# Two transformer layers on one core: scores of one head pair and maxima of another in one visit to the PSUM banks

## The chip, the cores and the metric

The kernel runs on one core of a Trainium2 chip. The metric is the time of one execution on the device in microseconds, median of three runs. The core has five engines with a queue each: TensorE (PE; its weight loads are listed as PEld), VectorE (DVE), ScalarE (ACT), GpSimd (POOL) and SyncE (SP), which here issues most DMAs. Each engine takes its own instructions in order, and semaphores tie the engines together.

## The reference

Two layers on x of 2048 rows and 640 columns. Each layer is attention with a sliding window of 256 keys (32 heads of 20 columns) and a feed-forward with squared ReLU (1536 wide):

```python
def _A_ref(x, wqkv, wo):
    H = 32; Dh = D // H; W = 256
    ...
    scores = jnp.einsum("bhqd,bhkd->bhqk", q, k) * (Dh ** -0.5)
    mask = (idx[:, None] - idx[None, :] >= 0) & (idx[:, None] - idx[None, :] < W)
    scores = jnp.where(mask[None, None], scores, -1e9)
    p = _softmax(scores, axis=-1)
    o = jnp.einsum("bhqk,bhkd->bhqd", p, v)
    return (...o...) @ wo
def _B_ref(x, w1, b1, w2, b2):
    h = jnp.einsum("bsd,df->bsf", x, w1) + b1
    r = jnp.where(h > zero, h, zero)
    return jnp.einsum("bsf,fd->bsd", r * r, w2) + b2
...
x = x + _A_ref(_layernorm(x), A_wqkv, A_wo)
x = x + _B_ref(_layernorm(x), B_w1, B_b1, B_w2, B_b2)
x = x + _A_ref(_layernorm(x), A_wqkv, A_wo)
x = x + _B_ref(_layernorm(x), B_w1, B_b1, B_w2, B_b2)
```

## The kernel before

The rows are cut into units of 256; two layers make 16 units (`NU`), numbered u. A unit is u % 8 == 0 at the start of a layer, where no earlier keys exist. Every dense product is done on fp16 high and low halves: `mm3` (L322) sums three products for each chunk of 128, high times high, high times low, low times high. Dense work of a unit is the query and key projection (`stage_qk`), the value projection (`stage_v`), the output projection (`stage_o`) and the feed-forward (`stage_f`), in that order of data. Dense groups accumulate in one of two PSUM tiles of the tag "mm"; ACT or DVE empties a tile before it is used again. The values and the small transposes use the same two tiles.

Attention works by head pairs: 16 pairs in a unit, 8 quads of two pairs. One head of a pair sits in rows 0 to 63, the other in rows 64 to 127 (index e), so a score matmul is a 64x64 tile of PE. Six PSUM banks, `bb6`, three for each e, hold scores. They are used twice for each quad:

- `max_quad` (L616) computes the scores of a quad with queries on the partitions (L652, or L667 at the start of a layer) and posts eight DVE reductions (L632), which add a mask, take the row maxima and write the masked scores back in place into the banks. A reduction shows as two DVE instructions, the reduction and a read of the accumulator into `mx`. The maxima are turned by a DMA (`max_cross`) or by PE (`max_out`) and appended as two extra rows of the queries. Maxima run `LEAD` = 3 quads ahead of the scores that need them.
- `exp_quad` (L736) computes the scores with keys on the partitions and with the maximum already subtracted by the two extra rows (L756, or L764 without 64-column tiles). ACT takes the exponential of each bank (L778: six of 512 columns a quad) into SBUF tiles `pt`, and POOL zeroes what the window excludes (L793, L797).

`pv_quad` (L813) multiplies the masked exponentials with the values (L827), four heads side by side in 32-column tiles; ACT copies the result to `ot` (L839) and SP stores it to DRAM (L844). `load_o` reads it back in the layout that the output projection needs and divides by the row sums.

The order of each engine's instructions is written by the program itself: a planner with its own clock `now` posts a job for each ACT, DVE, POOL and SP instruction with an estimated cost, and PE's work is emitted as the planner's clock goes on. `together` (L1092) walks a unit's quads: scores of quad n, a share of the dense stream, maxima of quad n+3 and then values of quad n, the rest of the share. Before scores or maxima it goes on with dense work until the jobs that use the banks (`bbjobs`) have ended by the planner's clock. `flow` (L1156) does the same for the first unit. In the last two units part of the dense work is held back (`CARRY`, `KEEP`) for the stretch behind the last values, where the output projection waits for `load_o`.

## Time and profile before

| | |
|---|---|
| median of 3 runs | 1591.49 us (1591.14 to 1591.74) |
| the profiled execution | 1590.84 us, of which the span of its instructions is 1589.1 us |
| PE | 1558.1 us busy |
| DVE, ACT, POOL | 983.8, 735.2, 599.5 us busy |
| granted TensorE clock, mean | 0.997 |

The page names an instruction by its line, engine and operation, then the tile it writes and the tiles it reads. Busy time of PE includes the modelled end of each matmul; two groups' starts are the better measure of what a group costs. A bracket behind a timeline row gives the idle time of that engine just ahead of the row, and whose signal ended it.

### The profile page before, as it was taken

How to read it: one execution, taken by the hardware profiler on the slowest of the kernel's cores; microseconds unless marked ns; L12 is line 12 of the kernel's file. 1: busy time of each engine (PE TensorE's matmuls, PEld its weight loads, DVE VectorE, ACT ScalarE, POOL GpSimd, SP SyncE). 2: the span in 40 equal slices, each digit the busy share in tenths (PEclk: the TensorE clock that was granted, in tenths of full speed). 3: DMA queues.
4: the chain of work that ended last, by engine and by line, in shares of the span. 5: the costliest groups of instructions: out<-in, count | busy, mean ns of one | idle time of the engine just before them, and what ended most of it. 6: DMA issues, size and time to landing. Idle time of an engine off the chain costs nothing.

```text
span 1589.1 us, 52465 instructions
## 1 busy us (share of the span) xinstructions
PE 1558.1 (98%) x21534; PEld 1167.5 (73%) x21534; DVE 983.8 (62%) x3253; ACT 735.2 (46%) x1593; POOL 599.5 (38%) x1291
## 2 busy tenths in 40 slices
PE   8989999999999999999999999999999999999999
PEld 7666767777777777778777777777777777776767
DVE  8787665656756656665566656557665665756432
ACT  4555535444453444535343453544545345454522
POOL 1234424334252443525323352442535235353512
PEclk9999999999999999999999999999999999999999
DMA  9763243362533525343362535434343352441020
GB/s 273 206 181 100 70 121 81 100 129 52 121 87 103 110 65 130 69 127 84 97 133 57 122 83 123 92 88 111 69 123 83 98 123 64 111 83 58 29 67 18
DMA packets 243209, 160.44 MB, mean 101 GB/s; under 512 B 91160, under 2 KB 226712, under 8 KB 242968
## 3 DMA queue, kind: packets, MB, share of 16 engines
q1 hardware_dynamic: 236600, 147.58, 38.8%
q10 hardware_dynamic: 6368, 9.50, 2.0%
q8 instruction: 169, 2.77, 0.7%
q14 instruction: 72, 0.59, 0.1%
HBM read 84.68 MB, written 52.95 MB: 87 GB/s over the span
## 4 chain that ended last, share of the span: by engine, by line
PE 91%; DVE 3%; ACT 2%; DMA 2%; SPq 1%; issue 1%; POOL 0%; ACTq 0%; DVEq 0%; POOLq 0%
PE acc L327 70%; PE pv L827 11%; PE bb L652 5%; PE bb L756 5%; DVE bb L632 1%; ACT pt L778 1%; DMA o<-ot 0%; PE bb L764 0%; DMA ov<-o 0%; PE bb L667 0%; SPq L688 0%; DVE qd L509 0%; DVE mx L632 0%; DMA qt<-qk 0%; DMA qk<-qd 0%
## 5 line engine op out<-in xcount | busy, mean ns | idle before, releaser
L778 ACT ACTIVATE pt<-bb 128x512 f32<-128x512 f32 (+1 forms) x736 | 376.9, 603 | 221.8 <-PE bb L756 198.9
L632 DVE CUSTOM_DVE_ANT_0 bb<-bb,maskq 128x320 f32<-128x320 f32 x896 | 409.2, 525 | 95.3 <-PE bb L652 88.6
L793 POOL TENSOR_SCALAR_AFFINE_SELECT pt<-pt 128x256 f32<-128x256 f32 x448 | 188.0, 422 | 558.1 <-ACT pt L778 545.3
L327 PE MATMUL acc<-y,w_s 128*128 128x256 f16 x2880 | 327.9, 273 | 2.1 <-ACT y L377 1.4
L327 PE MATMUL acc<-w_s,hh 128*128 128x320 f16 x2304 | 326.2, 299 | 0.0
L327 PEld LDWEIGHTS <-w_s 128*128 128x128 f16 x2880 | 276.6, 98 | 53.5 <-issue 17.7
L327 PEld LDWEIGHTS <-hh 128*128 128x128 f16 x2304 | 220.5, 98 | 98.4 <-issue 11.5
L327 PEld LDWEIGHTS <-wq_s 128*128 128x128 f16 x2400 | 230.0, 98 | 46.5 <-issue 13.8
L327 PE MATMUL acc<-yT,wq_s 128*128 128x256 f16 x2250 | 259.5, 273 | 2.1 <-DVE qd L509 0.7
L797 POOL TENSOR_SCALAR_AFFINE_SELECT pt<-pt 128x256 f32<-128x256 f32 x512 | 213.5, 438 | 89.2 <-ACT pt L778 87.6
L1012 DVE TENSOR_TENSOR hh<-r,hh 128x256 f16<-128x256 f32 x192 | 94.6, 513 | 213.2 <-ACT hh L1009 206.0
L827 PE MATMUL pv<-pt,vt 128*32 128x128 f32 (+1 forms) x3840 | 191.9, 330 | 0.7 <-POOL pt L797 0.6
L1006 POOL TENSOR_TENSOR r<-r 128x256 f32<-128x256 f32 x192 | 114.3, 615 | 169.5 <-ACT r L1002 167.2
L839 ACT COPY ot<-pv 128x256 f32<-128x256 f32 x128 | 47.8, 373 | 270.0 <-PE pv L827 266.1
L632 DVE DVE_READ_ACCUMULATOR2_ANT mx<- 128x1 f32 x1024 | 145.9, 143 | 0.0
L327 PE MATMUL acc<-wo_s,od 128*128 128x320 f16 x960 | 140.0, 301 | 3.8 <-ACT od L910 3.2
L827 PEld LDWEIGHTS pv<-pt,vt 128*32 128x32 f32 x3840 | 105.4, 109 | 42.1 <-POOL pt L797 6.9
L327 PE MATMUL acc<-wq_s,yT 128*128 128x320 f16 x900 | 131.8, 299 | 1.0 <-DVE y L378 0.5
L327 PEld LDWEIGHTS <-od 128*128 128x128 f16 x960 | 91.7, 98 | 48.7 <-issue 6.9
L1002 ACT ACTIVATE r<-acc,b1s 128x256 f32<-128x256 f32 x192 | 80.9, 473 | 95.9 <-PE acc L327 95.1
L327 PEld LDWEIGHTS <-yT 128*128 128x128 f16 x900 | 85.7, 98 | 39.2 <-issue 6.8
L364 POOL TENSOR_TENSOR bmv<-bmv,neghalf 128x1 f32<-128x1 f32 x64 | 44.2, 696 | 141.3 <-DVE bmv L358 140.8
(95 smaller groups left out, 1225.5 us busy)
## 6 DMA issues: line engine op xcount, KB each, us to landing
qt<-qk SPq DMA_DIRECT2D x30, 480.0 KB
kt<-qk SPq DMA_DIRECT2D x30, 480.0 KB
qk<-qd SPq DMA_DIRECT2D x17, 640.0 KB
o<-ot SPq DMA_DIRECT2D x256, 42.0 KB
od<-o SPq DMA_DIRECT2D x14, 640.0 KB
qk<-yl SPq DMA_DIRECT2D x13, 640.0 KB
qk<-qd SPq DMA_DIRECT2D x17, 320.0 KB
xt<-in_A_x_dram SPq DMA_DIRECT2D x16, 320.0 KB
```

Of the source, the lines that this page charges most:

```text
L327: nc.tensor.matmul(acc, lhs(a, c), rhs(b, c), start=(k == 0), stop=(k == 3 * nk - 1))
L632: nc.vector.tensor_tensor_reduce(out=v, in0=v, in1=mask, scale=1.0, scalar=-3.0e38, op0=ALU.add, op1=ALU.max, accum_out=accum[e, w]),
L652: nc.tensor.matmul(flat[e][rows, o:o + b - a], qt[r, p, i * P + 64 * h:i * P + 64 * (h + 1)], kt[r, p, a + to:b + to], start=True, stop=Tr ...
L756: nc.tensor.matmul(bb[e][rows, k, o + a:o + b], kt[r, 2 * qd + j, ko + 64 * h:ko + 64 * (h + 1)], qt[r, 2 * qd + j, q0 * P + a:q0 * P + b] ...
L778: nc.scalar.activation(box["pt"][:, :o], bb[e][:, k, :o], AF.Exp, scale=SCALE / (QS * QS))
L793: nc.gpsimd.affine_select(out=m, in_=m, pattern=[[0, 2], [-1, P]], compare_op=ALU.is_gt, fill=0.0, base=0, channel_multiplier=1)
L797: nc.gpsimd.affine_select(out=m, in_=m, pattern=[[0, 2], [1, P]], compare_op=ALU.is_ge, fill=0.0, base=0, channel_multiplier=-1)
L827: nc.tensor.matmul(pv[32 * jj:32 * (jj + 1), q0 * P:(q0 + qn) * P], vf[:, c:c + 32], pj[:, j, :], start=(k == 0), stop=(k == len(steps) - ...
L839: nc.scalar.copy(ot[:, qd % 2], pv)
L1002: nc.scalar.activation(box["r"], acc[:, f, :], AF.Relu, bias=b1s[:, f0 + f:f0 + f + 1], scale=1.0 / (YS * WS))
L1006: nc.gpsimd.tensor_tensor(box["r"], box["r"], box["r"], op=ALU.mult)
L1012: nc.vector.tensor_sub(hh[:, 1, f, :], box["r"], hh[:, 0, f, :])
```

## The change

The step is now a visit, one pair long instead of a quad. A visit computes the scores of one pair into columns 0 to 767 of the three banks of each e (0 to 383 at the start of a layer), and right behind them the scores for the maxima of a pair six ahead, into columns 768 to 1407 (1024 to 1407 at the start of a layer). A visit posts two exps of up to 768 columns and four reductions. The reductions write into two small SBUF tiles, `junk`, instead of the banks. At every second visit, ahead of the scores, come the values of the quad that the two visits before completed.

```diff
-    def max_quad(n):
+    GP = 2 * GQ
+    def max_pair(n):
...
+            def put():
+                j = junk[len(junked) % 2]
+                junked.append(0)
+                nc.vector.tensor_tensor_reduce(out=j[:, :cols], in0=v, in1=mask, scale=1.0, scalar=-3.0e38,
+                                               op0=ALU.add, op1=ALU.max, accum_out=acc)
...
-                p, at = 2 * qd + j, 5 * Q * w
-                cuts = sorted({0, 5 * Q, *(z - at for z in (512, 1024) if 0 < z - at < 5 * Q)})
+            places = [(i, 6 * P + 5 * Q * i) for i in range(2)]
+            for i, at in places:
+                cuts = sorted({0, 5 * Q, *(z - at for z in (1024,) if 0 < z - at < 5 * Q)})
...
-    def exp_quad(n):
+    def exp_pair(n, quad):
...
+        steps = [(3, cur, P, 1, 1), (2, cur, 0, 0, 2)]
+        if u % NG:
+            steps = [(1, prev, P, 0, 2), (0, prev, 0, 0, 1)] + steps
+        cols = sum(s[4] for s in steps) * P
...
-                    box["pt"] = sb.tile([P, 512], F32, name="pt", tag="pt", bufs=6)
-                    nc.scalar.activation(box["pt"][:, :o], bb[e][:, k, :o], AF.Exp, scale=SCALE / (QS * QS))
+                box["pt"] = sb.tile([P, 768], F32, name="pt", tag="pt", bufs=4)
+                nc.scalar.activation(box["pt"][:, :cols], bb[e][:, :cols], AF.Exp, scale=SCALE / (QS * QS))
...
     def pv_quad(n, quad):
+        need(*[j for _, ms in quad for j in ms])
...
-            ots[u] = sb.tile([P, 2, T], F32, name="ot", bufs=2)
+            ots[u] = sb.tile([P, 2, T], F32, name="ot", bufs=1)
...
-    LEAD = GQ + 1
+    LEAD = 6
...
+        for k, n in enumerate(ns):
+            m = ms[k] if k < len(ms) else None
...
+            work(k, Want(*wants, bank=full))
+            if full:
+                pv_quad(*hang.pop())
+            if not hang:
+                hang.append((n // 2, []))
+            banks()
+            exp_pair(n, hang[0][1])
             if m is not None:
-                max_quad(m)
+                max_pair(m)
...
-    QKC, VC, OC, FCST, LNC, CARRY, KEEP, MID = 16.4e3, 8.2e3, 8.2e3, 39.2e3, 1.2e3, 15e3, 20e3, 8e3
+    QKC, VC, OC, FCST, LNC, CARRY, KEEP, MID = 16.4e3, 8.2e3, 8.2e3, 39.2e3, 1.2e3, 20e3, 24e3, 8e3
...
-    spin(14)
+    spin(13)
...
-    spin(7)
+    spin(4)
...
-    run(some(dense, 10e3), stage_o(NU - 1), some(dense, 4e3))
+    flush(dense)
+    run(some(dense, 7e3), stage_o(NU - 1), some(dense, 4e3))
```

`flow` is rewritten by pairs in the same way, and `stage_o` may now wait for a `load_o` that the planner has not yet posted. Apart from attention, the first block of the first unit's query projection and the first block of the last feed-forward take all chunks of one product ahead of the next product, and their transposed operand is cut into four tiles, so that each product depends only on the pieces it reads:

```diff
-    def mm3(acc, lhs, rhs, nk, ns, then=None):
+    def mm3(acc, lhs, rhs, nk, ns, then=None, whole=0):
...
+        terms = ((0, 0), (0, 1), (1, 0))
+        if whole:
+            terms = [[t] for t in (terms if whole == 1 else terms[::2] + terms[1:2])]
+        for c, part in ([(c, part) for part in terms for c in range(nk)] if whole else [(c, terms) for c in range(nk)]):
...
+    def pieces_of(*tiles):
+        return lambda a, c, n, m: tiles[2 * a + c // 3][:, c % 3:c % 3 + n, m]
```

On PE, in the middle of the program, a quad's maxima (L652) were followed by its values (L827) and then by dense work (L327). `bb_133` and `bb_134` are the banks of e = 0 and 1, `kt` keys, `qt` queries, `vt` values:

```order
L652 LDWEIGHTS qt
L652 MATMUL bb_134<-kt_86,qt 64x192
L827 MATMUL pv<-pt,vt_93 32x256 [waits DVE_49,Pool_49]
L827 MATMUL pv<-pt,vt_93 32x256 [waits Pool_49]
L827 MATMUL pv<-pt,vt_93 32x256 x2
L827 MATMUL pv<-pt,vt_92 32x128 [waits Pool_49] x2
```

Now the values (L823 of the changed kernel) are followed by a pair's scores (L777):

```order
L823 MATMUL pv<-pt,vt_91 32x256 [waits DVE_49,Pool_49]
L823 MATMUL pv<-pt,vt_91 32x256 [waits Pool_49] x3
L823 MATMUL pv<-pt,vt_90 32x128 x4
L823 MATMUL pv<-pt,vt_93 32x128 x3
L823 MATMUL pv<-pt,vt_93 32x128 [waits Pool_49]
L823 MATMUL pv<-pt,vt_92 32x256 x4
L777 LDWEIGHTS kt_86
L777 MATMUL bb_133<-qt,kt_86 64x192
```

The values moved from behind the maxima to ahead of the scores, and the scores of the visit run straight on into its maxima (L678), with no dense work and no wait between:

```order
L777 MATMUL bb_133<-qt,kt_87 64x192
L777 LDWEIGHTS kt_87
L777 MATMUL bb_134<-qt,kt_87 64x192
L678 LDWEIGHTS qt
L678 MATMUL bb_133<-kt_87,qt 64x256
```

On DVE, the reductions of a quad stood in one row of eight behind a wait for PE:

```order
L632 ISA bb_133,mx<-bb_133,maskq 128x320 [waits PE_49]
L632 ISA mx 128x1
L632 ISA bb_134,mx<-bb_134,maskq 128x320 [waits PE_49]
L632 ISA mx 128x1
L632 ISA bb_133,mx<-bb_133,maskq 128x320 [waits DVE_49]
```

Now four stand together (L658), other work goes between the fours, and the first two wait for ACT:

```order
L1016 TENSOR_TENSOR hh<-r,hh 128x256 [waits Activation_49]
L658 ISA junk_135,mx<-bb_133,maskq 128x320 [waits Activation_49]
L658 ISA mx 128x1
L658 ISA junk_136,mx<-bb_134,maskq 128x320 [waits Activation_49]
L658 ISA mx 128x1
L658 ISA junk_135,mx<-bb_133,maskq 128x320 [waits DVE_49]
```

What moved is the signal that releases the first reduction of each bank: from PE's to ACT's, whose exp of the same visit reads the same banks.

## The prediction

> **What bounds the kernel now.** I read the page's first part first, then the windows, then the PE timeline of a stretch in the middle, then the waits.

> ```profile
> span 1589.1 us, 52465 instructions
> PE 1558.1 (98%) x21534; PEld 1167.5 (73%) x21534; DVE 983.8 (62%) x3253; ACT 735.2 (46%) x1593; POOL 599.5 (38%) x1291
> 0.00:160.00 160.00, 144.69 (x1638) 107.06 (x1639) 126.22 (x417) 84.51 (x173) 44.53 (x91) 0.98 0.69 189
> 160.00:240.00 80.00, 77.07 (x1149) 56.36 (x1148) 52.32 (x169) 36.28 (x78) 29.74 (x68) 0.98 0.40 96
> 240.00:1370.00 1130.00, 1129.97 (x16077) 851.32 (x16076) 698.44 (x2332) 525.10 (x1142) 441.15 (x961) 1.00 0.42 97
> 1370.00:1500.00 130.00, 124.05 (x1936) 90.24 (x1935) 81.02 (x282) 64.52 (x143) 61.87 (x132) 1.00 0.28 68
> 1500.00:1590.00 90.00, 82.28 (x741) 62.51 (x741) 25.80 (x56) 24.78 (x59) 22.25 (x40) 1.00 0.12 39
> ```

> A window row gives its length, then busy time of PE, PEld, DVE, ACT and POOL. The reader is to see that between 240 and 1370 us PE is busy for 1129.97 of 1130 us. PE's idle time lies at the two ends: 15.3 us before 160, 2.9 up to 240, 6.0 in 1370 to 1500, and 7.7 after 1500 (each the length less the first number). These 32 us are all that better waiting can give. DVE and ACT, which the change relieves most, are at 62% and 46%; in the long middle a faster DVE buys nothing. The first 160 us differ: DVE is busy for 126 of them.

> A busy PE may still lose time between its kinds of work, so the middle is read from the timeline: start, then the busy time of the group. One group's start to the next group's start is its price.

> ```profile
> 701.44 0.75 PE L756 MATMUL bb<-qt,kt 62*64 62x192 f16 x32
> 702.12 3.16 PE L327 MATMUL acc<-wq_s,yT 128*128 128x320 f16 x22
> 705.12 2.20 PE L327 MATMUL acc<-wo_s,od 128*128 128x320 f16 x15
> 707.25 0.76 PE L652 MATMUL bb<-kt,qt 60*64 60x256 f16 x38
> 707.94 1.51 PE L827 MATMUL pv<-pt,vt 128*32 128x256 f32 x32
> 709.38 4.25 PE L327 MATMUL acc<-wo_s,od 128*128 128x320 f16 x30
> ```

> A quad's scores (L756) cost 0.68 us, its look-ahead scores for maxima (L652) 0.69, its values (L827) 1.44. Dense matmuls cost 3.00 / 22 = 0.136 us each, and the 15 ahead of 707.25 take 2.13 instead of 2.04: 0.09 us to leave the dense shape. Nothing here waits; it is work.

> **The change, part by part.** Changes of shape: before, one quad is dense, scores, dense, maxima, values, dense. After, per two visits: dense, values, scores+maxima, dense, scores+maxima. PE leaves its dense shape twice per quad either way; "maxima to values" and "values to dense" give way to "values to scores" and "maxima to dense". Priced by the rows above these are equal, so 0. Scores to maxima has no row; both are 64-column tiles on 60 or 62 rows, so I take 0, with 0.09 us as the upper end, the row for leaving a shape. [...]

> Matmuls: the new places (columns 768 and 1088 of a three-bank row) need 18 maxima matmuls a pair, 36 a quad instead of 38. At (0.68 + 0.69) / 70 = 0.02 us a matmul the most that this gives is 0.04 us a quad, the least nothing. I take 0.027, times the 112 quads with 64-column tiles: **-3 us** (0 to -4.4).

> Turn-round of the banks: today maxima wait for all exps of a quad.

> ```profile
> PE bb L652 <- ACT pt L778: 8.9, 8, 2.7
> PE bb L756 <- DVE mx L632: 0.6, 3, 0.2
> 201.47 0.75 PE L756 MATMUL bb<-qt,kt 62*64 62x192 f16 x32
> 202.31 3.05 ACT L778 ACTIVATE pt<-bb 128x512 f32<-128x512 f32 x6 [3.13 <-PE bb L756]
> 204.93 0.27 PE L652 MATMUL bb<-kt,qt 60*64 60x256 f16 x1 [2.70 <-ACT pt L778]
> ```

> In all 8.9 us, eight times, where too little dense work lay between the two (here none). After the change scores and maxima go to different columns in one visit, so this wait is gone: **-8.9 us**. In its place the next visit's scores wait for this visit's exps and reductions. Its length:

> ```profile
> L778 ACT ACTIVATE pt<-bb 128x512 f32<-128x512 f32 x704 | 367.7, 612 | 221.8 <-PE bb L756 198.9 <-PE bb L764 15.7 <-DVE x L1040 4.0
> L778 ACT ACTIVATE pt<-bb 128x256 f32<-128x256 f32 x32 | 10.8, 398 | 0.0
> L797 POOL TENSOR_SCALAR_AFFINE_SELECT pt<-pt 128x256 f32<-128x256 f32 x512 | 213.5, 438 | 89.2 <-ACT pt L778 87.6 <-POOL pt L797 0.4
> 709.00 0.53 DVE L632 CUSTOM_DVE_ANT_0 bb<-bb,maskq 128x320 f32<-128x320 f32 x1
> 709.45 0.53 DVE L632 CUSTOM_DVE_ANT_0 bb<-bb,maskq 128x320 f32<-128x320 f32 x1
> 711.69 0.48 DVE L938 SCALAR_TENSOR_TENSOR x<-acc,x 128x320 f32<-128x320 f32 x1
> 712.09 0.87 DVE L353 BATCH_NORM_STATS2 bst<-x 128x6 f32<-128x320 f32 x2
> ```

> 256 more columns cost an exp 612 - 398 = 214 ns, so one of 768 takes 0.83 us; six of 512 follow each other at 3.05 / 6 = 0.51 us, so two of 768 at 0.72. A reduction that writes PSUM follows the last at 0.45 us; a DVE instruction of as many columns that reads PSUM and writes SBUF lets the next start after 0.40 (711.69 to 712.09). The new reductions write SBUF: I take 0.40, with 0.45 as the other end. Signalling: the scores that start at 201.47 end at 202.15, the exp starts at 202.31, 0.16 us later.

> In the order the first two reductions of a visit stand behind the visit's exps (waits Activation). So after a visit's last matmul: 0.16, exps until 0.16 + 0.72 + 0.83 = 1.71, 0.16, three reductions, 0.16: 3.2 us. If exps and reductions ran side by side, 0.16 + 4 x 0.40 + 0.16 = 1.9. Against it stand the slots of dense matmuls between visits. In the middle the shortest is 23 of 0.136 = 3.1 us once a unit, the next 28 (3.8 us); with other work in the queues I take 0.13 us a unit, **+1.5** (0 to 3). In the last two units some nine slots have 15 to 20 matmuls, 2.0 to 2.2 us, and lack up to 1.0 each: **+6** (0 to 9.4, the sum of what each lacks to 3.2). In the first unit slots of 15 of 0.109 = 1.6 us meet exps of 384 columns and reductions of 128 and 256, about 2.1 us by the same rows; seven such slots: **+1.5** (0 to 3).

> The values still wait for POOL: two masks behind each of the last pair's exps, 1.71 + 0.16 + 2 x 0.44 = 2.7 us after the visit, and values follow at least 28 dense matmuls (3 us) later: 0, covered by that dense work. In the last unit this cover is thin, which the range holds.

> The ends: the first block of the first projection now takes its operands in the order in which they are made, and so does the last feed-forward's first block.

> ```profile
> 10.80 0.39 PE L327 MATMUL acc<-yT,wq_s 128*128 128x256 f16 x2 [0.24 <-ACT wq_s L259]
> 11.82 0.94 PE L327 MATMUL acc<-yT,wq_s 128*128 128x256 f16 x7 [0.63 <-DVE wq_s L260]
> 1545.31 0.27 PE L327 MATMUL acc<-y,w_s 128*128 128x256 f16 x1 [1.40 <-ACT y L377]
> 1546.17 1.03 PE L327 MATMUL acc<-y,w_s 128*128 128x256 f16 x8 [0.60 <-DVE y L378]
> ```

> The DVE halves (0.63 and 0.60) are needed 10 matmuls (1.1 us) later and so hidden, and part of the 1.40, since the last block starts from a piece of the operand: **-2** (-1.2 to -2.6).

> DVE in the first 160 us: about 150 reductions fall there, each 0.05 us shorter, 7.5 us of DVE's 126. Only part stands where PE waits for DVE: **-3** (0 to -7.5).

> The single output buffer of the values (two before) makes the copy of every second quad wait for the stores of the quad before, issued a quad's 12 us earlier:

> ```profile
> 709.54 0.37 ACT L839 COPY ot<-pv 128x256 f32<-128x256 f32 x1 [2.49 <-PE pv L827]
> 709.94 1.35 SPq L844 DMA_DIRECT2D o<-ot  x4
> ```

> All four are issued within 1.8 us of the copy, so 10 us remain to land: 0. Without that cover ACT would stand, and PE two groups later.

> **The sum**: -3 - 8.9 + 1.5 + 6 + 1.5 - 2 - 3 = -7.9 us on the span of 1589.1, so 1581.2. The profiled run took 1590.84, 1.7 us over its span, and the median is 1591.49; taken off the median: **1584 us** (0.5% faster).

> **The rivals.** *Exp and reduction in one bank.* Columns 512 to 767 (exp) and 768 to 1023 (maxima) share a bank, and the order makes the second engine wait. A reduction at DVE's head, held 1.0 us by the first exp and 0.3 by the second, holds the evictions behind it too, whose banks the dense work needs. DVE's middle load is 698 of 1130 us, 7.4 of a quad's 12; two visits add up to 2.6 us and save 0.4, so on average DVE keeps up. But in the first 160 us some 30 visits of 1 us each bring 126 - 7.5 + 30 = 149 of 160. It decides where slots lie under 3.2 us: all new waits at their upper ends (15.4), no gain from DVE at the start and 7 us lost there, plus 0.5 us a unit for late evictions (6.5): -3 - 8.9 + 15.4 - 2 + 7 + 6.5 = +15, **1606 us**. For it: the waits in the order; against it: the room in the middle. [...]

> *Waits only change place*: the new waits eat the 8.9 and DVE's relief comes to nothing: -3 - 8.9 + 12 - 2 = -2, **1590 us**. For it: the ends have a fixed amount of dense work to cover with.

> *Scores to maxima costs a change of shape*: 0.09 us twice a quad, 112 x 0.18 = +20 on the sum: **1604 us**. Against it: both use 64-column tiles.

> *No new wait appears*: -3 - 8.9 - 2 - 5 = -19, **1572 us**, if the planner's spacing holds and DVE's relief counts at the start.

> **How the numbers follow.** Forecast 0.42 (its own range 1575 to 1588), no new wait 0.12, waits change place 0.14, the shared bank 0.27, the change of shape 0.05. About 0.2%, 3 us, is what a measurement of this kernel can tell from no change. Faster: 0.41 + 0.12 + 0.04 = 0.57; same: 0.01 + 0.09 = 0.10; slower: 0.27 + 0.05 + 0.01 = 0.33. The range takes in the bounds of both signs, from "no new wait" to the shared bank: 1570 to 1607.

> **What would show it.** Right: PE fully busy between 240 and 1370; no wait of maxima for exps; scores plus maxima 0.67 to 0.69 us a visit; reductions 0.40 us apart; waits of scores for reductions under 10 us in all, at the two ends. The shared bank shows as idle DVE ahead of reductions put down to ACT, and PE waiting in the middle; a change of shape as visits of 0.76 us or more. I am wrong if PE's idle time in the first 160 us grows, or if PE idles in the middle.

## The result and the profile after

The changed kernel takes **1633.09 us** (median of five runs, 1628.13 to 1636.51) against 1591.49: a ratio of 1.0256, 95% interval 1.0243 to 1.027. It is slower by 2.6%, where 0.5% faster was forecast, and 26 us above the upper end of the range. Its profiled execution took 1634.25 us, 1632.5 of it the span.

The windows of the changed kernel, columns as before (length, then PE, PEld, DVE, ACT, POOL busy; granted clock, DMA share, GB/s):

```profile
0.00:160.00 160.00, 132.83 (x1379) 93.93 (x1380) 117.00 (x391) 76.19 (x147) 31.63 (x75) 0.94 0.69 186
160.00:240.00 80.00, 76.24 (x1112) 56.65 (x1112) 44.46 (x157) 36.49 (x68) 32.46 (x70) 0.98 0.32 81
240.00:1370.00 1130.00, 1113.36 (x15664) 837.56 (x15662) 675.50 (x2296) 523.58 (x961) 431.00 (x947) 1.00 0.40 96
1370.00:1500.00 130.00, 123.65 (x1859) 89.53 (x1861) 76.73 (x273) 58.37 (x101) 50.35 (x116) 1.00 0.34 84
1500.00:1632.00 132.00, 120.15 (x1316) 90.12 (x1306) 50.61 (x140) 44.70 (x94) 42.73 (x84) 1.00 0.12 36
```

PE now idles in the middle: 1130 - 1113.36 = 16.6 us, where it had none. In the first 160 us it idles 27.2 us instead of 15.3, and its clock there is 0.94 instead of 0.98, which takes at most another 160 x 0.04 = 6.4 us (an estimate, as if PE had work all that time). DVE is not the busy engine: 117.00 us in the first 160 instead of 126.22, 675.50 in the middle instead of 698.44.

The spans differ by 43 us. Where these lie can be read from starts on PE's timeline (us from the span's start; e3 and e12 are experiments below):

| | before | after | e3 | e12 |
|---|---|---|---|---|
| first feed-forward matmul of unit 1 | 251.1 | 267.8 | 254.0 | 249.4 |
| the same of unit 12 | 1304.1 | 1338.7 | 1307.4 | 1299.8 |
| last matmul of the program | 1585.1 | 1628.5 | 1592.8 | 1581.3 |
| one unit in the middle | 96.58 | 98.16 | 96.48 | 96.18 |

So 16.7 us are lost ahead of the first row, 17.9 between the first two (1070.9 instead of 1053.0), and 8.8 behind.

The waits of the changed kernel (engine, tile and line that waited, whom for: us in total, times, longest):

```profile
DVE junk L658 <- ACT pt L794: 375.7, 380, 3.7
ACT pt L794 <- PE bb L678: 163.0, 153, 4.3
PE pv L823 <- DVE x L1045: 9.3, 12, 1.4
PE acc L330 <- DVE qd L526: 8.1, 11, 0.7
PE bb L777 <- DVE mx L658: 4.9, 11, 1.0
```

The first row is new. In the kernel before, of the 95.3 us that DVE stood idle ahead of its reductions of 320 columns, 1.1 were put down to an exp:

```profile
L632 DVE CUSTOM_DVE_ANT_0 bb<-bb,maskq 128x320 f32<-128x320 f32 x896 | 409.2, 525 | 95.3 <-PE bb L652 88.6 <-ACT r L1002 4.2 <-ACT pt L778 1.1
```

Now DVE stands 375.7 us with a reduction at the head of its queue that waits for an exp, 375.7 / 380 = 0.99 us each time. The last row is the wait that the prediction priced, scores waiting for reductions, and it is small. PE's large new waits are the third and fourth row: the values wait for the addition that empties the second feed-forward's bank (L1045), and the value projection waits for the second half of the query projection's eviction (L526). Within the middle they come to 8.2 and 7.4 us, ten times each: nearly all of the 16.6. One of them in the timeline (accumulator reads are left out):

```profile
719.88 0.47 PE L777 MATMUL bb<-qt,kt 62*64 62x192 f16 x16
720.19 0.46 PE L678 MATMUL bb<-kt,qt 60*64 60x256 f16 x18
720.58 3.45 PE L330 MATMUL acc<-yT,wq_s 128*128 128x256 f16 x30
720.83 1.51 ACT L794 ACTIVATE pt<-bb 128x768 f32<-128x768 f32 x2 [1.88 <-PE bb L678]
721.67 0.49 DVE L658 CUSTOM_DVE_ANT_0 junk<-bb,maskq 128x320 bf16<-128x320 f32 x1 [2.00 <-ACT pt L794]
722.38 0.49 DVE L658 CUSTOM_DVE_ANT_0 junk<-bb,maskq 128x320 bf16<-128x320 f32 x1 [0.20 <-ACT pt L794]
722.43 0.60 ACT L523 ACTIVATE qd<-acc 128x512 f16<-128x512 f32 x1
722.79 0.49 DVE L658 CUSTOM_DVE_ANT_0 junk<-bb,maskq 128x320 bf16<-128x320 f32 x1
723.20 0.49 DVE L658 CUSTOM_DVE_ANT_0 junk<-bb,maskq 128x320 bf16<-128x320 f32 x1
723.73 0.17 DVE L723 TENSOR_SCALAR mh<-mx 128x16 f16<-128x16 f32 x1
723.94 0.18 DVE L724 SCALAR_TENSOR_TENSOR mh<-mx,mh 128x16 f16<-128x16 f32 x1
724.04 0.68 DVE L526 SCALAR_TENSOR_TENSOR qd<-acc,qd 128x512 f16<-128x512 f32 x1
724.77 1.25 PE L330 MATMUL acc<-wq_s,yT 128*128 128x320 f16 x8 [0.75 <-DVE qd L526]
```

The eviction's first half (L523, ACT) is done at 723.03. Its second half needs DVE, but four reductions and the split of their maxima stand ahead of it. All are late, because the first reduction was held until 721.67, 1.1 us after its matmuls gave way to dense work at 720.58. PE, which has finished its 30 matmuls, waits 0.75 us for the bank.

### The profile page after: what moved, and what is told of

Its sections match the earlier page's. It is cut to its first block, busy times and chain, and to the rows that moved or that the text cites. A ratio compares the mean times of both kernels' runs of the same rounds, so it can differ in the third digit from the quotient of the medians.

```text
span 1632.5 us, 51742 instructions
## 1 busy us (share of the span) xinstructions
PE 1566.2 (96%) x21310; PEld 1167.8 (72%) x21310; DVE 964.3 (59%) x3253; ACT 739.3 (45%) x1369; POOL 588.2 (36%) x1291
## 5 line engine op out<-in xcount | busy, mean ns | idle before, releaser
L658 DVE CUSTOM_DVE_ANT_0 junk<-bb,maskq 128x320 bf16<-128x320 f32 x896 | 403.2, 488 | 354.6 <-ACT pt L794 349.0
L794 ACT ACTIVATE pt<-bb 128x768 f32<-128x768 f32 (+1 forms) x512 | 369.6, 768 | 212.1 <-PE bb L678 163.0
L330 PE MATMUL acc<-yT,wq_s 128*128 128x256 f16 x2160 | 252.8, 274 | 1.0 <-ACT wq_s L259 0.9
L823 PE MATMUL pv<-pt,vt 128*32 128x128 f32 (+1 forms) x3840 | 186.0, 330 | 17.0 <-DVE x L1045 9.3
L1016 DVE TENSOR_TENSOR hh<-r,hh 128x256 f16<-128x256 f32 x192 | 108.4, 577 | 136.4 <-ACT hh L1013 128.9
L823 PEld LDWEIGHTS pv<-pt,vt 128*32 128x32 f32 x3840 | 105.7, 110 | 71.8 <-issue 43.9
L777 PEld LDWEIGHTS <-kt 62*64 62x64 f16 x3568 | 70.5, 106 | 80.7 <-issue 62.4
L330 PEld LDWEIGHTS <-yT 128*128 128x128 f16 x864 | 81.5, 98 | 47.7 <-issue 13.0
L777 PE MATMUL bb<-qt,kt 62*64 62x192 f16 (+1 forms) x3568 | 108.9, 236 | 6.3 <-DVE mx L658 4.9
```

Source lines behind the costliest of these rows:

```text
L330: nc.tensor.matmul(acc, lhs(a, c), rhs(b, c), start=(k == 0), stop=(k == 3 * nk - 1))
L658: nc.vector.tensor_tensor_reduce(out=j[:, :cols], in0=v, in1=mask, scale=1.0, scalar=-3.0e38, op0=ALU.add, op1=ALU.max, accum_out=acc)
L777: nc.tensor.matmul(bb[e][rows, o + a:o + b], kt[r, p, ko + 64 * h:ko + 64 * (h + 1)], qt[r, p, q0 * P + a:q0 * P + b], start=True, stop=Tr ...
L794: nc.scalar.activation(box["pt"][:, :cols], bb[e][:, :cols], AF.Exp, scale=SCALE / (QS * QS))
L823: nc.tensor.matmul(pv[32 * jj:32 * (jj + 1), qs], vf[:, c:c + 32], box["pt"][:, part], start=(kb == kbs[0]), stop=(kb == kbs[-1]), skip_gr ...
L1016: nc.vector.tensor_sub(hh[:, 1, f, :], box["r"], hh[:, 0, f, :])
```

## The experiments

Two theories stood at the start. **A**: reductions wait for the visit's exps because both read one tile, and what stands behind them on DVE comes late. **B**: the first 160 us are lost through the single output buffer `ot`. Later a theory **C** was added, on the placing of transposes and values in the first unit (e5). Runs of the kernel before, made together with the experiments, gave medians of 1591.9 to 1592.7.

### e1 and e2: the wait itself

The shared tile cannot simply be split: 768 and 640 columns do not fit into two and one of the kernel's banks of 512 columns. So the maxima windows were cut to 256 columns in both runs, all in the third bank; e2 alone makes that bank a tile of its own.

```diff
-            places = [(i, 6 * P + 5 * Q * i) for i in range(2)]
+            places = [(i, 1024 + 4 * Q * i) for i in range(2)]          # e1; e2 has (i, 4 * Q * i)
...
+    bm2 = [ps.tile([P, 512], F32, name=f"bm{e}") for e in range(2)]     # e2; bb{e} has two banks
...
```

> The changed kernel, but each maxima window is 256 columns instead of 320 (the last 64 keys of every window of units 1 to 7 and 9 to 15 are left out of the maximum), and both windows lie in the third bank of the shared tile, which no exp reads. A control for the next run. The maxima matmuls fall from 0.39 to 0.31 us a visit: 224 visits x 0.08 = 17.6 us less work for PE; a reduction falls from 0.41 to about 0.34 us. Theory A (the reductions stand behind the visit's exps because both read one tile, and the late evictions behind them make PE wait): PE still waits 1 to 2 us a unit in the middle, DVE still stands 300 us or more ahead of reductions put down to the exps, time 1605 to 1618. Rival (bank): if the wait came from the bank that exps and maxima share, it is gone here already, since the maxima now have a bank of their own: DVE's idle time put down to the exps under 100 us, time 1575 to 1592.

> As the run before (256-column windows, the same banks and columns), but the maxima lie in a tile of their own. The planner sees the same jobs, so the order should be nearly that of the run before; only the waits differ. Theory A: DVE's idle time put down to exps falls from over 300 us to under 100, PE idles under 4 us in 240 to 1370, and the time is 25 to 40 us under the run before: 20 of it in the middle, 5 to 20 in the first 160 us. Rival B (the first 160 us lose 20 us through the single output buffer, not through the held reductions): 16 to 22 us under the run before, all of it in the middle. Rival C (PE's waits in the middle are for DVE's load or the planner's spacing, whatever the reductions wait for): within 5 us of the run before.

e1: 1623.23 us, ratio 1.0177 (1.016 to 1.0194). e2: 1587.78 us, ratio 0.9953 (0.9937 to 0.997): 35.5 us less, for the same matmuls and the same reductions. Waits of e1, the first row over the whole span, the other two between 240 and 1370 us:

```profile
DVE junk L658 <- ACT pt L794: 394.9, 403, 3.9
PE pv L823 <- DVE x L1045: 13.6, 10, 1.4
PE acc L330 <- DVE qd L526: 5.4, 10, 0.5
```

And e1's window there:

```profile
240.00:1370.00 1130.00, 1110.65 (x15068) 836.88 (x15066) 639.51 (x2324) 526.08 (x965) 430.54 (x956) 1.00 0.41 96
```

The same two views of e2. The first row is the reductions' largest wait, and no row of a reduction names exps any more:

```profile
DVE junk L659 <- PE bm L679: 197.9, 173, 3.9
PE pv L824 <- DVE x L1046: 3.8, 11, 0.4
```

```profile
240.00:1370.00 1130.00, 1124.67 (x15334) 851.91 (x15335) 649.16 (x2349) 533.34 (x975) 442.63 (x971) 1.00 0.42 98
```

The bank rival falls with e1: there no exp reads the maxima's bank, and DVE still stands 394.9 us for exps. The wait goes with the tile, not with the bank. e2 removes it, and PE's idle time in the middle drops from 19.4 to 5.3 us; the expectation was under 4. The split takes two more ties away: in e1 exps waited 164.2 us for the maxima matmuls of their visit, and scores 6.4 us for reductions (L777); in e2 the first wait is 2.0 us and the second is gone. So its 35.5 us belong to all three; e3 below deals with the first alone. Of e2's gain 10.5 us lie ahead of unit 1's feed-forward, 16.4 up to unit 12's and 7.9 behind, by the same starts as in the table. B, as an explanation for all of the start, falls with the 10.5. Rival C of that expectation falls too (the C of e5 is another). e1 missed its own number: 17.6 us of matmuls were to go, and it is 9.9 us under the changed kernel. A visit's maxima matmuls take 0.33 us from their start to the next group's, instead of 0.39, not the 0.31 expected, so 224 x 0.06 = 13 us went; and the two waits in the middle grew from 15.6 to 19.0 us in all, probably because shorter matmuls leave less cover for the same late evictions.

Whether an exp and a reduction would wait for each other in one bank, if each had a tile of its own there, no run here shows.

### e3: the same wait, but known to the planner

```diff
-            bbjobs.append(post("D", 60 + 1.047 * cols, put, prio=urgency["turn"]))
+            bbjobs.append(post("D", 60 + 1.047 * cols, put, *exps[e:e + 1], prio=urgency["turn"]))
...
-                max_pair(m)
+                max_pair(m, bbjobs[-2:])
...
```

> The changed kernel whole; the planner is told that a reduction can start only when the visit's exp on the same row of banks has ended, so that it can put evictions ahead of a held reduction. The waits in the program stay. Theory A in its form 'order' (the loss is the evictions' place in DVE's queue): the PE waits for the second feed-forward's additions and the projection's evictions in the middle go from 16.6 to under 6 us, the first 160 us gain 3 to 8: 1610 to 1620. Rival in its form 'length' (the turn-round of 3.06 us itself is too long for the slots, so a better place does not help): within 5 us of 1633.

Measured: 1597.92 us, ratio 1.0027 (1.0017 to 1.0037). One dependency in the planner's model, with not one wait taken out of the program, brings back 35 of the 42 us, more than expected. A wait of e3, and its window in the middle:

```profile
DVE junk L658 <- ACT pt L794: 331.7, 376, 4.0
```

```profile
240.00:1370.00 1130.00, 1129.65 (x15931) 852.84 (x15933) 684.79 (x2327) 527.50 (x968) 436.80 (x963) 1.00 0.42 98
```

DVE still stands 331.7 us for exps. PE has next to no idle time in the middle now (1129.65 of 1130), so the length of the turn-round was not the loss there. The same place of the program in e3's timeline (accumulator reads and the second reduction are left out):

```profile
699.52 1.51 ACT L794 ACTIVATE pt<-bb 128x768 f32<-128x768 f32 x2 [1.88 <-PE bb L678]
700.37 0.49 DVE L658 CUSTOM_DVE_ANT_0 junk<-bb,maskq 128x320 bf16<-128x320 f32 x1 [2.00 <-ACT pt L794]
701.48 0.48 DVE L658 CUSTOM_DVE_ANT_0 junk<-bb,maskq 128x320 bf16<-128x320 f32 x1
701.89 0.69 DVE L526 SCALAR_TENSOR_TENSOR qd<-acc,qd 128x512 f16<-128x512 f32 x1
702.50 0.48 DVE L658 CUSTOM_DVE_ANT_0 junk<-bb,maskq 128x320 bf16<-128x320 f32 x1
702.63 1.25 PE L330 MATMUL acc<-wq_s,yT 128*128 128x320 f16 x8
```

The first reduction is held by the same 2.00 us. But the planner now knows that reductions run late, and puts the eviction ahead of the last of them and of the split: L526 starts 2.37 us after the first exp instead of 3.21, and PE does not wait.

A planner that knows more could also have spaced the visits differently. In the unit that starts at 464.1 us in the changed kernel and at 446.9 in e3, PE's order is the same up to both places where PE waited; only behind them do two of the sixteen visits stand earlier, by 12 and 15 dense matmuls. On DVE, L526 stands one reduction and the split earlier there, and L1045 one instruction (L460). So it is the place of the evictions in DVE's queue that ends these two waits. e2 and e3 are about equally good: with the 13 us of matmuls that it leaves out, e2 would stand near 1601 us by estimate.

### e4: the output buffer

```diff
-            ots[u] = sb.tile([P, 2, T], F32, name="ot", bufs=1)
+            if u == 0 and qd % 4 == 2:
+                ots[u] = hraw[:, KC * T:(KC + 2) * T].rearrange("p (a n) -> p a n", a=2)
+            else:
+                ots[u] = sb.tile([P, 2, T], F32, name="ot", bufs=1)
```

> The changed kernel whole; in the first unit every second pair of quads copies its values into a free part of the staging area, so that two output buffers alternate there as before the change. Theory B (the single output buffer holds ACT, and with it weights and evictions, in the first 160 us): 8 to 20 us of the 20 lost there come back, 1613 to 1625. Theory A (held reductions are the cause there too): only the wait of 4.6 us of the copy and the PE wait of 1.4 behind it go, 1628 to 1633.

Measured: 1630.66 us, ratio 1.0225 (1.021 to 1.024), 2.4 us under the changed kernel. In the changed kernel's ACT timeline one copy waited (work between the first two rows is left out):

```profile
78.71 0.37 ACT L834 COPY ot<-pv 128x256 f32<-128x256 f32 x1 [2.10 <-PE pv L823]
87.80 0.37 ACT L834 COPY ot<-pv 128x256 f32<-128x256 f32 x1 [4.60 <-DMA o<-ot]
88.06 0.44 ACT L597 ACTIVATE vt<-acc 128x320 f32<-128x320 f32 x1
88.39 1.36 ACT L259 ACTIVATE w_s<-w_s 128x640 f16<-128x640 f32 x2
```

The eviction of values (L597) and a weight's conversion (L259) were held with it. In e4 that wait is gone, and with it PE's wait of 1.4 us behind it. So the single buffer does hold ACT, but it does not explain the start: the time is the one expected by A. Even the 2.4 us are barely clear of noise: the runs of e4 (1628.63 to 1631.55) lie within those of the changed kernel.

### e5 to e8: what is left on e3's base

e5 places a transpose or a quad's values in the first unit only when a PSUM tile is free; e6 adds e4's second buffer; e7 sets two constants back; e8 undoes the writing of reductions to SBUF.

```diff
+            if not done(wants) or kind in ("v", "r") and len(banks2) > 1 and not any(b and done(b) for b in banks2):   # e5, e6
...
-    ..., CARRY, KEEP, MID = ..., 20e3, 24e3, 8e3
+    ..., CARRY, KEEP, MID = ..., 15e3, 20e3, 8e3                                                                        # e7
...
-                nc.vector.tensor_tensor_reduce(out=j[:, :cols], in0=v, ...
+                nc.vector.tensor_tensor_reduce(out=v, in0=v, ...                                                        # e8
```

> The kernel of the run e3 (the planner knows that reductions wait for exps), and in the first unit the planner places a transpose of maxima or a quad's values only when a PSUM bank for it is free, and dense work until then. Theory C (in the first 110 us PE loses 5 to 6 us because transposes and values stand ahead of dense work and wait for a bank): the waits of values for the DVE halves of the transposed maxima and for evictions (0.8, 0.4, 0.8, 1.1, 0.8 us) and of transposes for evictions (0.6, 1.3) mostly go, 3 to 6 us under e3's 1597.9. Rival: DVE's evictions are late whatever stands next on PE, so dense work meets the same waits: within 2 us of 1597.9.

> As the run before, with two output buffers in the first unit. If the single buffer's cost (2.5 us in e4) adds to the others: 1.5 to 4 us under the run before. If it counted in e4 only because ACT was late there for another reason (the held evictions): within 1 us of the run before.

> The kernel of e3 with the two amounts of dense work that are kept for the last unit and for behind its last pair as they were before the change (15 and 20 us of PE work instead of 20 and 24). Theory: the tail's loss against before (about 5 us after 1370 in e3) is the turn-round of 3.1 us a visit against slots that share a fixed amount of dense work, so the amounts only move waits: 1595 to 1601. Rival: the amounts are set wrongly for the new visits, and the old ones win the loss back: 1590 to 1594.

> The kernel of e3 with one part of the change undone: a reduction writes its product back to PSUM in place, as before the change. By my term for DVE's relief the reductions follow each other at 0.45 us instead of 0.41, the turn-round grows by 0.15 us a visit, and the first 160 us and the tail lose 1 to 5 us: 1599 to 1603. Rival: neither DVE nor the turn-round decides once the evictions stand ahead of the reductions, so nothing changes: within 1 us of 1597.9.

| | median us | ratio to before, 95% interval |
|---|---|---|
| e5 | 1595.27 | 1.0019 (1.001 to 1.0027) |
| e6 | 1594.54 | 1.0017 (1.0008 to 1.0026) |
| e7 | 1599.58 | 1.0048 (1.0031 to 1.0065) |
| e8 | 1607.90 | 1.0097 (1.0084 to 1.011) |

e5 is 2.7 us under e3, less than expected and with overlapping intervals. In its profiled execution unit 1's feed-forward starts 4.7 us earlier than in e3, and 4.1 us are lost again behind unit 12's; but that first start also differs by 1.9 us between e3 and e7, whose edits concern the last units only. So C is likely worth a few microseconds, but these runs do not settle it. e6 adds nothing that can be told: on this base the single buffer no longer shows. e7 moves the time by 1.7 us, within its expectation: the dense work at the end is only moved about. e8 is the surprise: writing in place costs 10 us. Of the span's 9.8 us, 2.8 lie ahead of unit 1's feed-forward, 4.3 up to unit 12's (a unit in the middle takes 96.92 instead of 96.48 us) and 2.7 behind. The two groups of L658 in e8, then in e3 (durations min/median/max in ns):

```profile
L658 DVE DVE_READ_ACCUMULATOR2_ANT mx<- x1024: 128/141/145, 31.0 to 1506.5; 128x1 f32 x171
L658 DVE CUSTOM_DVE_ANT_0 bb<-bb,maskq x896: 473/500/535, 92.2 to 1506.0; 128x320 f32<-128x320 f32 x180
```

```profile
L658 DVE DVE_READ_ACCUMULATOR2_ANT mx<- x1024: 71/83/89, 30.9 to 1495.1; 128x1 f32 x171
L658 DVE CUSTOM_DVE_ANT_0 junk<-bb,maskq x896: 427/487/493, 90.7 to 1494.7; 128x320 bf16<-128x320 f32 x180
```

A reduction itself is 13 ns longer in place and the read behind it 58 ns. Over 1024 reductions that adds up: DVE is busy for 1009.2 us instead of 964.7, and what stands behind a reduction comes later. That would fit the cause found above. But no row of PE's waits in the middle names more than 0.2 us (a pause under 0.15 us is in no such row), and PE's idle time there grows only from 0.35 to 2.3 us; how the 10 us come about stays open.

### e9 to e12: the clock, a second unknown wait, and a version that is faster

```diff
+                for k in range(18 if u == i == h == 0 else 0):
+                    nc.tensor.matmul(acc[:, :P], ident, ident, start=True, stop=True)              # e9, e10, e11
...
-            ex = post("A", 50 + 0.834 * cols, power, prio=urgency["turn"])
+            ex = post("A", 50 + 0.834 * cols, power, wait=wait, prio=urgency["turn"])              # e10, e12: 300 (first unit 200)
...
+    ..., CARRY, KEEP, MID = ..., 24e3, 20e3, 8e3                                                   # e11
+    ..., CARRY, KEEP, MID = ..., 20e3, 24e3, 11e3                                                  # e12
...
+    run(some(dense, 10e3), stage_o(NU - 1), some(dense, 4e3))                                      # e12
```

> The kernel of e6 with 18 matmuls of the identity put into the pause ahead of the first output projection (PE idle 4.53 us there in e6, and the granted clock 0.67 and 0.65 in the ten us from 120). Their sums are overwritten, nothing waits for them, and the planner is not told. Theory (a pause of PE lowers its clock for the next five to ten us, which is part of what the waits of the first 160 us cost): the clock in those ten us is over 0.9 and the time 1.5 to 3.4 us under e6. Rival (the clock falls there for another reason, the load or chance): the clock stays at 0.65 to 0.7, and the time within 1 us of e6.

> As the run before, and the planner is told one more thing that the trace shows: the exps of a visit wait for the visit's maxima matmuls as well, so they start about 0.3 us later than it reckoned. Theory A carried on (every wait that the planner does not know costs PE): 0.5 to 3 us under the run before, most of it in the first unit and after 1370. Rival (0.3 us is within what the slots cover): within 1 us of it.

> As e9, with 24 us of dense work carried into the last unit (20 before) and 20 kept behind its last pair (24 before). If the tail's loss is slots that are too short, longer ones in the last unit give 1 to 3 us, and the clock after 1460 stays at 1.0. If a fixed amount of dense work is only moved about: within 2 us of e9, with PE's pauses at other places after 1370.

> The kernel of e10 without the 18 identity matmuls, with 11 us of dense work instead of 8 ahead of the last unit's first output projection and 10 us instead of 7 ahead of the last one (10 is the value of the kernel before the change). In e10 PE pauses there for 1.61 and 2.05 us at 1450 to 1456 and 2.79 us at 1527, each followed by five to ten us at a granted clock of 0.57 to 0.75. Theory (long pauses cost themselves and the clock behind them): these pauses shrink below 1 us and the time falls 3 to 7 us under e10's 1591.6, to 1585 to 1589, faster than the kernel before. Rival (the dense work at the end is a fixed amount, so the pauses come back behind the projection): within 2 us of e10.

| | median us | ratio to before, 95% interval |
|---|---|---|
| e9 | 1597.02 | 1.0023 (1.0014 to 1.0031) |
| e10 | 1591.59 | 0.9994 (0.9985 to 1.0002) |
| e11 | 1608.90 | 1.0106 (1.009 to 1.0121) |
| e12 | 1586.89 | 0.9961 (0.9947 to 0.9975) |

Windows of 5 us around the first output projection in e6, then in e9:

```profile
120.00:125.00 5.00, 1.27 (x5) 0.46 (x6) 4.78 (x11) 1.66 (x4) 2.33 (x4) 0.67 1.13 264
125.00:130.00 5.00, 5.00 (x26) 3.08 (x25) 0.32 (x1) 0.51 (x2) 0.00 (x0) 0.65 0.98 174
```

```profile
120.00:125.00 5.00, 3.43 (x28) 2.68 (x27) 4.01 (x10) 0.92 (x2) 1.56 (x3) 1.00 1.13 294
125.00:130.00 5.00, 3.15 (x24) 2.06 (x21) 0.12 (x1) 0.46 (x1) 0.00 (x0) 1.00 1.07 194
130.00:135.00 5.00, 2.95 (x12) 1.73 (x13) 4.42 (x18) 1.93 (x3) 0.43 (x1) 0.57 0.65 197
```

PE's timeline behind that, in e6, then in e9:

```profile
131.85 4.23 PE L330 MATMUL acc<-wo_s,od 128*128 128x320 f16 x30 [1.45 <-DVE x L939]
132.05 6.90 PE L330 MATMUL acc<-wo_s,od 128*128 128x320 f16 x30 [3.90 <-DVE x L942]
```

The 18 matmuls kept the clock at 1.00 in these ten us, so the pause (4.53 us in e6) did lower it; that half of the theory holds. The time did not fall (1597.02 us against 1594.54, with overlapping intervals): PE reached its next wait earlier. The projection's first addition starts at 131.51 us in e9 and 131.31 in e6, so something other than PE sets it, and PE waits 3.90 us for it instead of 1.45. On DVE that addition stands behind the last halves of the projection's operand (L911), which wait 5.37 us for ACT (L908); in e6, where they wait 4.89 us, ACT waits there 5.5 us for what the profile calls a DMA. And the low clock has only moved: in e6 the 30 matmuls of these rows take 4.23 us, in e9 6.90, at a clock of 0.57 in its third window. A gain ahead of a fixed event is given back at it.

e10 tells the planner of a second wait. The row `ACT pt L794 <- PE bb L678` above says that exps wait for the maxima matmuls behind their own scores. Told of that, the planner brings a unit from 96.48 to 96.18 us and the time 5.4 us under e9, more than the 3 expected (against e6, which is e9 without the 18 matmuls, it is 3.0). It was expected in the first unit and after 1370; it lies ahead of unit 1's feed-forward (3.6 us) and in the middle (2.6), and behind unit 12's 1.8 us are lost. PE had no idle time to speak of in the middle of e9 (1129.48 of 1130 busy), so that this is the cause of e3 a second time is argued from the edit, not seen in a wait. e11 loses 11.9 us against e9, all behind unit 12: with more work carried into the last unit PE idles 20.9 us behind 1370 instead of 13.1, which neither theory had.

e12 is faster than the kernel before by 0.39% and than the changed one by 2.8%. Two of its windows:

```profile
240.00:1370.00 1130.00, 1130.00 (x15975) 853.13 (x15974) 667.35 (x2338) 528.43 (x974) 433.62 (x964) 1.00 0.41 98
1370.00:1500.00 130.00, 126.67 (x1944) 93.71 (x1943) 76.04 (x271) 67.24 (x126) 62.51 (x138) 1.00 0.26 64
```

Its gain over e10 was expected at 3 to 7 us and is 4.7. It lies in the last units (281.5 us from unit 12's feed-forward start to the last matmul instead of 286.1), where the window from 1370 to 1500 now runs at full clock instead of 0.97. The pauses between 1450 and 1456 are gone; the one at 1527 is not, PE idles 3.35 us at 1536 instead. Which of the three edits did it was not separated.

## Why the prediction was wrong

**The step that failed** is the sentence "on average DVE keeps up" and the price built on it. The forecast let new waits appear only as scores waiting for reductions, and priced the instructions held behind a reduction at nothing; the rival *Exp and reduction in one bank* named them and gave them 0.5 us a unit and 7 us at the start. They cost 1.6 us a unit in the middle, and at the start e3, which changes their place, brings back 13.9 of the 16.7 us. The mechanism had been seen, down to "holds the evictions behind it too"; it was given the smaller chance and under half its size, because DVE's load was weighed instead of the question which instruction stands behind the held one and when PE needs it. DVE, busy for 59% of the span, was late with each of the two evictions ten times in the middle. How long a reduction is held had been sized rightly: 1.0 us by the first exp, and 0.99 was measured. What holds it had not: the rival named the bank, and e1 and e2 show the tile. And the planner was taken for something that spaces work well, when its model did not have the wait that the order already showed: e3 changes only that model and brings back 35 us.

Point by point:

- *Changes of shape 0* and *matmuls -3*: together about right, apart not. A unit of e3, where PE hardly waits, takes 96.48 us against 96.58, and 0.10 x 14 = -1.4 for both. But the bursts themselves gave nothing: in the rows above scores and maxima take 719.88 to 720.58, 0.70 us a visit, so 1.40 for two visits against 0.68 + 0.69 = 1.37 for a quad before. That lies just above the 0.67 to 0.69 forecast, and far from the 0.76 of the rival with a change of shape. That scores to maxima costs nothing was the author's estimate, and no row of the kernel before shows that turn; the 0.70 is for the two together. What became shorter lies in the dense stretches, and no run here shows why.
- *Maxima waiting for exps -8.9*: gone, as predicted; no such row is left.
- *Turn-round 3.2 us*: the length is right. In the rows above the maxima end at 720.58 and the last reduction at 723.69, 3.1 us. Its price as scores' waits (+9 in all) was too high: scores waited 4.9 us (L777) and 1.5 us (L784, the form without 64-column tiles) for reductions. The price that counted was the other one.
- *Ends -2*: the sixteenth dense matmul starts 0.8 us earlier and the 0.60 us wait of the last feed-forward is gone, but its 1.40 stays: about -1.4.
- *DVE relief -3*: reductions follow each other at 0.41 us, as said, but PE did not get it in the changed kernel. On e3's base the part is worth 10 us (e8): 2.8 at the start, near the term, and 7 in the middle and at the end, where the sum had nothing.
- *Single output buffer 0*: off by about 2.4 us (e4). The cover of "10 us to land" rested on a quad of 12 us. In the first unit the next copy was due at 83.20, 4.5 us after the one at 78.71, and waited 4.60 us for the stores.
- *Not in the sum at all*: the lower clock behind PE's pauses, at most 6.4 us in the first 160 by the estimate above.

What would show it had been listed rightly: idle DVE ahead of reductions put down to ACT, and PE idle in the middle. Both came.

## What to carry to other kernels

When a change adds a wait at the head of an in-order engine, go through the few instructions behind it in the order listing and ask for each who needs it next; the engine's load does not answer that. Where a planner or a cost table sets the order, check that it knows every wait that the built program has: two that it did not know cost 35 and some 3 to 5 us here, and telling it took a few lines each. What two engines read is better put into a tile for each, not only into a bank for each: e1, with a bank for each in one tile, has DVE standing 394.9 us for exps, and e2, with a tile for each, has no such wait.

## What the runs showed of the hardware

```profile
130.00:140.00 10.00, 5.00 (x33) 2.59 (x22) 7.20 (x18) 5.18 (x9) 2.52 (x4) 0.66 1.06 233
100.00:120.00 20.00, 16.02 (x227) 10.55 (x227) 13.31 (x49) 11.51 (x23) 3.51 (x9) 0.91 0.44 129
106.23 1.81 PE L330 MATMUL acc<-yT,wq_s 128*128 128x256 f16 x15
111.83 3.38 PE L330 MATMUL acc<-yT,wq_s 128*128 128x256 f16 x15
```

The first window holds one pause of 4.99 us, from 130.4 us on; over these ten us the clock is 0.66, and it fell at 132.3 us, 1.9 us into the pause. The second holds no pause over 1.50 us, only several in a row, and its clock is 0.91; it fell at 111.8, and the group at 111.83 takes 3.38 us, the one at 106.23 only 1.81.

The clock records of the kernel before and of the changed one show 1.0 or 0.5 and nothing between. Within the spans nine stretches are at 0.5: three in the kernel before, from 70.2, 118.0 and 206.8 us, each 3.4 us long; and six in the changed kernel, from 36.7, 74.3, 87.9, 111.8 and 163.0 us, each 3.4 us long, and from 132.3, 6.8 us long. In the 3.4 us ahead of them PE was busy for 1.98, 1.11 and 1.65 us, and for 1.67, 1.72, 1.50, 1.71 and 1.54 us, and 1.48 ahead of the long one.

Ahead of a fall PE was busy for 1.98 of the 3.4 us at most, but these two traces draw no line. In the 3.4 us from 1452.6 in the kernel before, and from 53.8, 797.9 and 1524.9 in the changed one, PE was busy for 1.80, 1.80, 1.97 and 1.86 us, less than that 1.98, and the clock stayed at 1.0 behind them. Busy time of PE includes modelled ends, so these figures are rough.
